# Attention and a spectral filter on one core: the filter's last feature products with the constants as weights, and results stored as whole blocks

## The chip, the cores and the metric

The program runs on one core of a Trainium2 chip. TensorE (PE) multiplies matrices, VectorE (DVE) and ScalarE (ACT) do elementwise work, GpSimd (POOL) and SyncE (SP) mostly issue DMAs. The metric is the device time of one execution in microseconds (us). It was 641.86 us in the median of three runs (641.53 to 643.83).

## The reference

Two independent results lie side by side in the output. The left half is attention of 16 heads of 28 features over 2048 positions, with one shared key and value head. The right half is a filter: a real two-dimensional Fourier transform, a product with complex weights, and the inverse transform.

```python
q = (x @ wq).reshape(B, S, 16, 28).transpose(0, 2, 1, 3)   # S = 2048, D = 448
k, v = x @ wk, x @ wv
p = softmax(einsum("bhqd,bkd->bhqk", q, k) * 28 ** -0.5)
a = (einsum("bhqk,bkd->bhqd", p, v)).transpose(0, 2, 1, 3).reshape(B, S, 448) @ wo

X = rfft2(x2) * (w_r + 1j * w_i)        # over positions and features
b = irfft2(X, s=(2048, 448))
out = concatenate([a, b], axis=-1)
```

## The kernel before

**Attention.** After a first phase (projections, the filter's forward products) the program is one long loop over 256 *steps*. A step is 128 keys against one group of four heads and 512 queries; 16 steps make a group, 16 groups make all. A step has four *scores* (`score`, L1100: keys as weights, 512 queries going through, one PSUM bank each), four exponentials on ACT (`exps`, L1117: a bank to a tile `p` in SBUF, from a pool of `P_BUFS` tiles), and four *value products* (`values`, L1132: 32 columns of the array each, two instructions per product). Value products of several steps are issued in one *batch*; `size` makes it 4 steps when other work is waiting and 2 when none is. All of a batch's tiles `p` must be there before it begins.

**Other work.** The loop puts *units* of other work between scores (`fill`): W units (`wo_mm`, L1020: the output projection, four pieces of three matmuls), and for the last part of the filter z units (L942) and y units (L961). A unit takes one of the seven PSUM banks that the scores also use, and holds it until DVE has copied the result out. A z unit multiplies four point blocks of the filtered spectrum with position constants `fi` (inverse transform over positions, eight instructions in float32); DVE copies its bank to SBUF (L948). A y unit is the inverse transform over features: four products of 113 feature constants (`cs3`), where the *points* z are the weights (128 columns) and the constants go through (113 columns), in float32, two instructions each. DVE then forms sums and differences in five operations (L966 to L975) and SP stores 128 output rows (L977). There are eight blocks q of points, with two z units and two y units each.

**What sets the order.** The order of every engine is fixed when the program is built. A planner (`clk`, `after`, `vector`, and the loop at L1189) walks through the loop with an estimated clock for PE, ACT and DVE and estimated costs per piece (the last numbers in `return [(0.88, go)]` and in `after(clk["pe"] + 1.2, 0.72, out, b)`), and writes down at each moment what its estimate allows: a score when a bank is free, a unit when its quota allows, the value products when their tiles are ready and 7 further scores (`LEAD`) are out or no bank is free. So a changed cost changes the order of everything behind it.

**Memory.** `X` (28.25 KB in each partition) holds the spectrum while DVE transforms it; it lies in a pool that is open for the whole program. After it is stored to `t2`, its space is carved up by hand for the buffers of the z and y units (`carve`, L912). The constants `cs3` are loaded into a tile of their own at the loop's start (L694).

Of the kernel before, what the change touches and what calls it, by code (L numbers as in the profile page):

```python
# [12 lines left out]
F32 = mybir.dt.float32  # L13
F32R = mybir.dt.float32r
# [3 lines left out]
ALU = mybir.AluOpType  # L18
# [4 lines left out]
S, D, H = 2048, 448, 16  # L23
# [5 lines left out]
NK = 4  # L29
SCALE = DH ** -0.5  # L30
BOUND = float(np.float32(40.0 / SCALE))
P_BUFS = 20
LEAD = 7
WARM = 8, 8
FIRST = 8
# [60 lines left out]
def kernel(ctx: ExitStack, tc: tile.TileContext, t: dict):  # L96
    nc = tc.nc
    mm = nc.tensor.matmul

    cp = ctx.enter_context(tc.tile_pool(name="cp", bufs=1))  # L100
    dp = ctx.enter_context(tc.tile_pool(name="dp", bufs=1, space=DRAM))
    qp = ctx.enter_context(tc.tile_pool(name="qp", bufs=1))
    fp = ctx.enter_context(tc.tile_pool(name="fp", bufs=2))
# [4 lines left out]
    vs = cp.tile([128, 16, 32], F32, name="vs")  # L108
    cvec = cp.tile([128, NG, NC], F32, name="cvec")
    bits = cp.tile([1, 1], F32, name="bits")  # L110
    X = cp.tile([128, 2, 32, 113], F32, name="X")
    t1 = dp.tile([64, 2, 2, 32 * 113], F32, name="t1")
    t2 = dp.tile([128, 2, 32 * 113], F32, name="t2")

    bank = [bp.tile([128, 512], F32, name=f"b{i}") for i in range(8)]
    turn = count()

    def view(b, *dims):
        n = int(np.prod(dims))
        names = "abc"[:len(dims)]  # L120
        return b[:, :n].rearrange(f"p ({' '.join(names)}) -> p {' '.join(names)}", **dict(zip(names, dims)))
# [4 lines left out]
    fc, xb, ff = {}, {}, {}  # L126
# [86 lines left out]
    with tc.tile_pool(name="f1", bufs=2) as f1[0], tc.tile_pool(name="w1", bufs=1) as w1, ExitStack() as ctx1:  # L213
# [124 lines left out]
        for j in range(NK):  # L338
            (xh_, xl_), w_ = split[0, j], wsp[j]
            if j == 0:  # L340
# [184 lines left out]
        for c in range(1, NC):  # L525
            for g in range(NG):
                n = 4 * (c - 1) + g
                m = None
                for j in range(NK):
# [4 lines left out]
                    m = add(PE, 0.2285 * (3 if j < 3 else 2), go, *split[c, j], users[-6] if j == 0 else None)  # L534
# [25 lines left out]
                if n in PLACES:  # L560
                    q = PLACES.index(n)
# [41 lines left out]
        for i in range(4):  # L603
            r = slice(32 * i, 32 * i + 32)
# [12 lines left out]
        with tc.If(rv > int(np.float32(BOUND).view(np.int32))), tc.tile_pool(name="g1", bufs=1) as g1:  # L617
# [10 lines left out]
            with tc.For_i(0, 64, 1) as n:  # L628
# [3 lines left out]
                for i in range(4):  # L632
                    r = slice(32 * i, 32 * i + 32)
# [11 lines left out]
            q, qh, ql = parts  # L645
# [14 lines left out]

    ap = ctx.enter_context(tc.tile_pool(name="ap", bufs=2))
    pp = ctx.enter_context(tc.tile_pool(name="pp", bufs=P_BUFS))
    V = nc.vector
    TT, STT = V.tensor_tensor, V.scalar_tensor_tensor

    clk = {"pe": 0.0, "dve": 4.0, "act": 0.0, "mode": "s", "new": False}
    free = [0.0] * 6 + [9.0]
# [4 lines left out]
    def after(when, dur, f, *a):  # L672
        heapq.heappush(events, (when, next(serial), dur, f, a))
# [16 lines left out]

    woh = ap.tile([128, NG, D], F32R, name="woh", bufs=1)
    wol = ap.tile([128, NG, D], F32R, name="wol", bufs=1)
    fc["cs3"] = ap.tile([113, 4, 113], F32, name="cs3", bufs=1)
    nc.gpsimd.dma_start(fc["cs3"], t["cs3"])  # L694

    late, held, early = {}, [None], deque()

# [208 lines left out]
                after(clk["dve"] + 3.0, 0.0, fft3_load, k)  # L906


    Xf = X.rearrange("p r n f -> p (r n f)")
    taken = [0]  # L910

    def carve(p, n):  # L912
        o = taken[0]
        taken[0] += n
        return Xf[:p, o:o + n]

    c2t = [carve(128, 904).rearrange("p (u j f) -> p u j f", u=2, f=113) for _ in range(2)]
    fit = [carve(128, 512).rearrange("p (j f) -> p j f", f=128) for _ in range(2)]
    zt = [[carve(113, 512).rearrange("p (r j n) -> p r j n", r=2, n=64) for _ in range(2)] for _ in range(2)]
    mt = [carve(128, 226).rearrange("p (k f) -> p k f", f=113) for _ in range(2)]  # L920
    y1t = [carve(128, 452).rearrange("p (k h f) -> p k h f", k=2, f=113) for _ in range(2)]
    yot = [carve(128, 452).rearrange("p (k f) -> p k f", f=113) for _ in range(2)]

    work = {"z": deque(), "w": deque()}
    cur, last_kind = [None], ["w"]
# [3 lines left out]
    def fft3_load(q):  # L929
        if q > 7:  # L930
            return
        nc.gpsimd.dma_start(c2t[q % 2].rearrange("p u j f -> p u (j f)"), t2[:, :, 452 * q:452 * q + 452])
        nc.gpsimd.dma_start(fit[q % 2], t["fi"][:, 4 * q:4 * q + 4])
        after(clk["dve"] + (10.0 if q < 2 else 6.0), 0.0, work["z"].extend, [z_unit(q, 0), z_unit(q, 1)])

    def z_unit(q, e):
        w = (113, 112)[e]

        def go(b):
            pz = view(bank[b], 4, 128)  # L940
            for j in range(4):
                mm(pz[:w, j], c2t[q % 2][:, e, j, :w], fit[q % 2][:, j], start=True, stop=True)  # L942
            if e == 1:
                after(clk["pe"] + 1.2, 0.0, fft3_load, q + 2)
            after(clk["pe"] + 1.2, 0.72, out, b)

        def out(b):
            V.tensor_copy(zt[q % 2][e][:w], view(bank[b], 4, 128)[:w].rearrange("p j (r n) -> p r j n", r=2))  # L948
# [3 lines left out]
        return [(0.88, go)]  # L952

    def y_unit(q, v):
        js = slice(2 * v, 2 * v + 2)

        def go(b):
            py = view(bank[b], 4, 113)
            ze, zo = zt[q % 2]
            for k, (z, w, r) in enumerate(((ze, 113, 0), (zo, 112, 0), (zo, 112, 1), (ze, 113, 1))):  # L960
                mm(py[:, k], z[:w, r, js], fc["cs3"][:w, k], start=True, stop=True)  # L961
# [150 lines left out]
    def exps():  # L1112

        while waiting and waiting[0][0] < 4 * done_steps + P_BUFS:
            i, b, at = waiting.popleft()
# [72 lines left out]
    n = size()  # L1188
    while done_steps < 256:  # L1189
# [10 lines left out]
        elif t_v <= clk["pe"] + 0.05 and (sc >= min(need + LEAD, 1024) or not soon):  # L1200
# [3 lines left out]
            n = size()  # L1204
# [15 lines left out]
        elif t_v <= min(free) or not more:  # L1220
# [3 lines left out]
            n = size()  # L1224
# [117 lines left out]
def _gather(oa, ob):  # L1342
    out = np.empty((1, S, 2 * D), np.float32)
    out[0, :, :D] = oa
    y = ob.reshape(32, 64, 4, 113).transpose(1, 0, 2, 3).reshape(S, 4, 113)
# [26 lines left out]
```

## Time and profile before

| | |
|---|---|
| median of three runs | 641.86 us |
| the profiled execution | 641.98 us |
| its span, first to last instruction | 640.1 us |
| PE, ACT, DVE busy | 633.5, 547.0, 333.3 us |
| scores L1100, 1024 instructions | 284.7 us busy, 411 ns each |
| value products L1132, 2048 instructions | 240.0 us busy, 597 ns each |
| exponentials L1117, 1024 instructions | 506.7 us busy, 768 ns each |
| y units L961, 128 instructions | 21.9 us busy |
| z units L942, 128 instructions | 16.6 us busy |
| granted TensorE clock | 0.999 |

Matmuls are pipelined: a matmul's duration in the trace is longer than the distance to the next, and a PE that is shown as busy may be waiting. So the distances between starts in the timeline say what a matmul costs, and the busy time of PE says little.

### The profile page before, as it was taken

To read this page: it belongs to the slowest core of one execution; us is meant where nothing else is said; L and a number is where in the kernel's file an instruction comes from. 1 tells how busy PE (TensorE), PEld (TensorE's weight loads), DVE (VectorE), ACT (ScalarE), POOL (GpSimd) and SP (SyncE) were. 2 spreads that over 40 slices of the span, in tenths; PEclk is the share of its full clock that TensorE was granted. 3 is DMA by queue.
4 is the path that set the end of the run, shared out by engine and by line. 5 is a ranking of instruction groups with operands and counts; after the bars stand their busy time and mean duration, and the time that the engine had idled before them with its cause. 6 is when DMAs were issued, how large, how long until landed. Compare 5 with 4: busy or idle time off the path is not lost.

```text
span 640.1 us, 11636 instructions
## 1 busy us (share of the span) xinstructions
PE 633.5 (99%) x4380; PEld 358.5 (56%) x4380; DVE 333.3 (52%) x687; ACT 547.0 (85%) x1100; POOL 89.1 (14%) x164
## 2 busy tenths in 40 slices
PE   9999999999999999999999999999999999999997
PEld 7877544444444456554446655655665655564445
DVE  5999615979897977896323222215334310320014
ACT  4644899999999998889999879878888987888991
POOL 1021131101121101010122020020301101020200
PEclk9999999999999999999999999999999999999999
DMA  8766587030334121124444231132415131130002
GB/s 299 255 164 166 134 239 244 18 68 17 97 105 102 42 68 47 32 67 150 151 141 139 64 91 36 49 111 88 115 61 143 32 82 32 50 93 1 19 0 87
DMA packets 29667, 62.41 MB, mean 98 GB/s; under 512 B 6798, under 2 KB 18415, under 8 KB 28645
## 3 DMA queue, kind: packets, MB, share of 16 engines
q1 hardware_dynamic: 21850, 40.36, 23.1%
q0 software_dynamic: 7328, 20.72, 10.8%
q8 instruction: 35, 0.57, 0.4%
q10 hardware_dynamic: 432, 0.57, 0.3%
q14 instruction: 22, 0.18, 0.1%
HBM read 29.63 MB, written 15.02 MB: 70 GB/s over the span
## 4 chain that ended last, share of the span: by engine, by line
PE 88%; ACT 0%; issue 0%; DVE 0%; ACTq 0%
PE b L1100 41%; PE b L1132 36%; PE b L1020 6%; PE b L961 2%; PE b L942 2%; PE b L1252 0%; PE b L163 0%; ACT yb L1035 0%; DVE yb L1038 0%; ACTq L1036 0%
## 5 line engine op out<-in xcount | busy, mean ns | idle before, releaser
L1117 ACT ACTIVATE p<-b 128x512 f32<-128x512 f32 x1024 | 506.7, 768 | 46.4 <-PE b L1100 45.4
L1100 PE MATMUL b<-qa,ka 128*128 128x512 f32 x1024 | 284.7, 411 | 0.5 <-PEq L617 0.5
L1100 PEld LDWEIGHTS b<-qa,ka 128*128 128x128 f32 x1024 | 182.1, 188 | 128.2 <-ACT p L1117 83.9
L1132 PE MATMUL b<-p,vs 128*32 128x512 f32 x2048 | 240.0, 597 | 0.0
L1132 PEld LDWEIGHTS b<-p,vs 128*32 128x32 f32 x2048 | 56.5, 109 | 120.9 <-issue 119.3
L986 DVE COPY qraw<-b 128x512 f32<-128x512 f32 x15 | 10.4, 692 | 82.0 <-PE b L1132 82.0
L1024 DVE COPY ya<-b 128x448 f32<-128x448 f32 x12 | 7.5, 624 | 65.1 <-PE b L1020 64.0
L991 POOL DMA_DIRECT2D sd<-qraw x15 | 8.8, 587 | 218.8 <-DVE qraw L986 218.8
L827 DVE SCALAR_TENSOR_TENSOR X<-w,X 128x226 f32<-128x226 f32 (+2 forms) x72 | 34.1, 473 | 2.4
L1000 POOL DMA_DIRECT2D R<-rd x60 | 30.2, 508 | 34.9 <-DMA rd<-rs 34.9
L966 DVE COPY X<-b 128x226 f32<-128x226 f32 x16 | 6.2, 390 | 45.3 <-ACT p L1117 43.9
L321 ACT ACTIVATE qraw<-b 128x512 f32<-128x512 f32 x16 | 9.4, 599 | 19.5 <-PE b L317 19.4
L948 DVE COPY X<-b 113x512 f32<-113x512 f32 (+1 forms) x16 | 11.1, 691 | 28.6 <-ACT p L1117 22.7
L317 PE MATMUL b<-xh,wqh 128*128 128x512 f32 x64 | 24.6, 416 | 0.4 <-DVE xh L265 0.4
L1008 DVE TENSOR_TENSOR qraw<-qraw,R 128x512 f32<-128x512 f32 x15 | 10.3, 685 | 26.7 <-DMA R<-rd 26.7
L317 PE MATMUL b<-xh,wql 128*128 128x512 f32 x64 | 23.0, 390 | 0.0
L1020 PE MATMUL b<-woh,oh 128*128 128x448 f32 x60 | 22.1, 369 | 0.0
L1020 PE MATMUL b<-wol,oh 128*128 128x448 f32 x60 | 22.0, 366 | 0.0
L1020 PE MATMUL b<-woh,ol 128*128 128x448 f32 x60 | 21.9, 366 | 0.0
L820 DVE SCALAR_TENSOR_TENSOR w<-X 128x113 f32<-128x113 f32 (+2 forms) x56 | 17.7, 353 | 0.1
L961 PEld LDWEIGHTS b<-cs,X 113*128 113x128 f32 (+1 forms) x128 | 16.8, 191 | 1.4
L317 PE MATMUL b<-xl,wqh 128*128 128x512 f32 x48 | 17.3, 391 | 0.0
(113 smaller groups left out, 511.4 us busy)
## 6 DMA issues: line engine op xcount, KB each, us to landing
qa<-qa SPq DMA_DIRECT2D x15, 512.0 KB
X<-t POOLq DMA_DIRECT2D x16, 452.0 KB, 5.4
xb<-xb SPq DMA_DIRECT2D x8, 512.0 KB
qa<-qh SPq DMA_DIRECT2D x60, 64.0 KB
qa<-ql SPq DMA_DIRECT2D x60, 64.0 KB
R<-rd POOLq DMA_DIRECT2D x60, 64.0 KB, 2.2
t<-bs SPq DMA_DIRECT2D x16, 226.0 KB
wf<-w POOLq DMA_DIRECT2D x8, 452.0 KB, 4.2
```

Source lines behind the costliest of these rows:

```text
L317: mm(pq[c, g], w[:, j, gs], x[:, j], start=(j == 0 and n == 0), stop=(j == 3 and n == 1))
L820: STT(out, y, sy, x, op0=ALU.mult, op1=ALU.add if c > 0 else ALU.subtract)
L827: todo(226 * n, lambda d=d, q=q: STT(both(d), t[0].rearrange("p r n f -> p r (n f)"), q, both(a), op0=ALU.mult, op1=ALU.add))
L942: mm(pz[:w, j], c2t[q % 2][:, e, j, :w], fit[q % 2][:, j], start=True, stop=True)
L948: V.tensor_copy(zt[q % 2][e][:w], view(bank[b], 4, 128)[:w].rearrange("p j (r n) -> p r j n", r=2))
L961: mm(py[:, k], z[:w, r, js], fc["cs3"][:w, k], start=True, stop=True)
L986: V.tensor_copy(o, bank[7])
L1000: nc.gpsimd.dma_start(R[32 * i:32 * i + 32], rd[i:i + 1].to_broadcast([32, CW]))
L1020: mm(p, x[c][:, g, s], w[:, g], start=(g == 0 and n == 0), stop=(g == NG - 1 and n == 2))
L1100: mm(bank[b], ka[:, kc * 128:(kc + 1) * 128], qa[c, g][:, h], start=True, stop=True)
L1117: nc.scalar.activation(p, bank[b], AF.Exp, scale=SCALE)
L1132: mm(bank[7][32 * i:32 * i + 32], vs[:, kc], pt.pop(4 * st + i), start=(kc == 0), stop=(kc == 15))
```

## The change

The operands of the y unit change places. Each feature constant (113 columns) becomes the weight, and the points (4 blocks of 64, 256 columns) go through. The products are in float32r instead of float32, and to keep the accuracy the constants and the points are each split into a high and a low part (`csh`, `csl`; `zh`, `zl`); one product becomes three (high by high, high by low, low by high). The two y units of a block q no longer take half of the points each, but half of the feature constants each. A unit has 6 instructions of 256 columns instead of 8 of 113.

DVE now writes two tiles per z unit (the high part by a copy, the low part by a subtraction), does three operations per y unit, and after the second unit of a block two operations of 512 columns that make the output blocks. SP stores two blocks of 113 x 512 for each q, each contiguous in DRAM; the host's `_gather` reorders accordingly.

`X` moves to a pool that is closed when the first z unit's data are loaded, and a new pool takes its space. The load of the constants moves from the loop's start to that moment, goes to a scratch tile, and two DVE operations make `csh` and `csl`. To make room, `P_BUFS` goes from 20 to 19. The planner's costs of the z and y units change.

```diff
-P_BUFS = 20
+P_BUFS = 19
...
-    X = cp.tile([128, 2, 32, 113], F32, name="X")
...
     pp = ctx.enter_context(tc.tile_pool(name="pp", bufs=P_BUFS))
+    xp = ctx.enter_context(ExitStack())
+    X = xp.enter_context(tc.tile_pool(name="xp", bufs=1)).tile([128, 2, 32, 113], F32, name="X")
...
-    fc["cs3"] = ap.tile([113, 4, 113], F32, name="cs3", bufs=1)
-    nc.gpsimd.dma_start(fc["cs3"], t["cs3"])
+    csh = ap.tile([113, 4, 113], F32R, name="csh", bufs=1)
+    csl = ap.tile([113, 4, 113], F32R, name="csl", bufs=1)
...
+    def fft3_open():
+        xp.close()
+        p3 = xp.enter_context(tc.tile_pool(name="p3", bufs=2))
+        for q in range(2):
+            fb["c2", q] = p3.tile([128, 2, 4, 113], F32, name="c2")
+            fb["fi", q] = p3.tile([128, 4, 128], F32, name="fi")
+            for e in range(2):
+                fb["z", q, e] = [p3.tile([113, 2, 4, 64], F32R, name=f"z{n}{e}") for n in "hl"]
+        cs = scratch()[:113, :452].rearrange("p (k f) -> p k f", k=4)
+        nc.gpsimd.dma_start(cs, t["cs3"])
+        todo(452, lambda: V.tensor_copy(csh, cs))
+        todo(452, lambda: TT(csl, cs, csh.bitcast(F32), op=ALU.subtract))
...
-            after(clk["pe"] + 1.2, 0.72, out, b)
+            after(clk["pe"] + 1.2, 1.4, out, b)
 
         def out(b):
-            V.tensor_copy(zt[q % 2][e][:w], view(bank[b], 4, 128)[:w].rearrange("p j (r n) -> p r j n", r=2))
+            pz = view(bank[b], 4, 128)[:w].rearrange("p j (r n) -> p r j n", r=2)
+            h, l = (x[:w] for x in fb["z", q % 2, e])
+            V.tensor_copy(h, pz)
+            TT(l, pz, h.bitcast(F32), op=ALU.subtract)
...
     def y_unit(q, v):
-        js = slice(2 * v, 2 * v + 2)
 
         def go(b):
-            py = view(bank[b], 4, 113)
-            ze, zo = zt[q % 2]
-            for k, (z, w, r) in enumerate(((ze, 113, 0), (zo, 112, 0), (zo, 112, 1), (ze, 113, 1))):
-                mm(py[:, k], z[:w, r, js], fc["cs3"][:w, k], start=True, stop=True)
-            after(clk["pe"] + 1.2, 1.2, out, b)
+            py = view(bank[b], 2, 256)
+            for k in range(2):
+                kind, e, r = ((0, 0, 0), (2, 1, 1), (1, 1, 0), (3, 0, 1))[2 * v + k]
+                w = (113, 112)[e]
+                zh, zl = (x[:w, r].rearrange("p j n -> p (j n)") for x in fb["z", q % 2, e])
+                for n, (c, z) in enumerate(((csh, zh), (csh, zl), (csl, zh))):
+                    mm(py[:113, k], c[:w, kind], z, start=(n == 0), stop=(n == 2))
+            after(clk["pe"] + 1.2, 2.65 if v else 1.25, out, b)
 
         def out(b):
-            py, m, y1 = view(bank[b], 4, 113), mt[v], y1t[v]
-            V.tensor_copy(m, py[:, 2:4])
-            TT(y1[:, :, 0], py[:, 0:2], m, op=ALU.add)
-            TT(y1[:, :, 1], py[:, 0:2], m, op=ALU.subtract)
-            free[b] = clk["dve"] + 0.1
-            after(clk["dve"], 0.8, last)
-
-        def last():
-            y1, yo = y1t[v], yot[v]
-            TT(yo[:, 0:2], y1[:, 0], y1[:, 1], op=ALU.add)
-            TT(yo[:, 2:4], y1[:, 0], y1[:, 1], op=ALU.subtract)
-            r0 = (2 * q + v) * 128
-            nc.sync.dma_start(t["ob"][r0:r0 + 128], yo)
-        return [(0.88, go)]
+            py = view(bank[b], 2, 256)[:113]
+            y = y1[v] = scratch()[:113, :768].rearrange("p (s n) -> p s n", s=3)
+            V.tensor_copy(y[:, 2], py[:, 1])
+            TT(y[:, 0], py[:, 0], y[:, 2], op=ALU.add)
+            TT(y[:, 1], py[:, 0], y[:, 2], op=ALU.subtract)
+            free[b] = clk["dve"] + (-1.3 if v else 0.1)
+            if v:
+                a, c = y1.pop(0), y1.pop(1)
+                for h, op in enumerate((ALU.add, ALU.subtract)):
+                    last(h, op, a, c)
+
+        def last(h, op, a, c):
+            yo = fp.tile([113, 2, 256], F32, name="yo", tag="bs")
+            TT(yo, a[:, :2], c[:, :2], op=op)
+            nc.sync.dma_start(t["ob"][q, h], yo)
+        return [(0.73, go)]
...
-    total = 12 * 4 * 0.605 + 32 * 0.88
+    total = 12 * 4 * 0.605 + 16 * (0.88 + 0.73)
...
-_OUTS = {"oa": (S, D), "ob": (S, 4, 113)}
+_OUTS = {"oa": (S, D), "ob": (8, 2, 113, 2, 256)}
```

**PE, y units late in the filter.** The rows are PE's instructions in program order, one row for each product or run of equal products; `b_` are PSUM banks, `qa` and `ka` the scores' operands. Before, two y units of one block stand in a loop of their own:

```order
L961 MATMUL b_79<-cs_1092,X 128x113 x4
L1100 MATMUL b_81<-qa_128,ka 128x512
L1100 MATMUL b_77<-qa_128,ka 128x512
L961 MATMUL b_78<-cs_1092,X 128x113 x4
L1100 MATMUL b_82<-qa_128,ka 128x512
L1100 MATMUL b_83<-qa_128,ka 128x512
L1100 MATMUL b_80<-qa_128,ka 128x512
```

The same place now, from the scores between the two y units on (scores are L1112, y products L971, z products L945):

```order
L1112 MATMUL b_78<-qa_1166,ka 128x512
L1112 MATMUL b_81<-qa_1166,ka 128x512
L971 MATMUL b_76<-zh_3747,csh 113x256
L971 MATMUL b_76<-zl_3748,csh 113x256
L971 MATMUL b_76<-zh_3747,csl 113x256
L971 MATMUL b_76<-zh_3745,csh 113x256
L971 MATMUL b_76<-zl_3746,csh 113x256
L971 MATMUL b_76<-zh_3745,csl 113x256
L1112 MATMUL b_77<-qa_1166,ka 128x512
L1112 MATMUL b_79<-qa_1166,ka 128x512
L945 MATMUL b_82<-fi,c_3749 112x128 x4
```

The unit has six products in place of four double ones, and behind the second y unit there now stands a z unit in the same batch.

**DVE, what takes the units out of their banks.** Before, two y units and the next block's two z units (`X` are the buffers carved from X):

```order
L966 COPY X<-b_80 128x226
L967 TENSOR_TENSOR X<-b_80,X 128x2x113
L968 TENSOR_TENSOR X<-b_80,X 128x2x113
L974 TENSOR_TENSOR X<-X 128x226
L975 TENSOR_TENSOR X<-X 128x226
L966 COPY X<-b_81 128x226
L967 TENSOR_TENSOR X<-b_81,X 128x2x113
L968 TENSOR_TENSOR X<-b_81,X 128x2x113
L974 TENSOR_TENSOR X<-X 128x226
L975 TENSOR_TENSOR X<-X 128x226
L948 COPY X<-b_79 113x512
L948 COPY X<-b_78 112x512
```

The same place now:

```order
L977 COPY w<-b_81 113x256
L978 TENSOR_TENSOR w<-b_81,w 113x256
L979 TENSOR_TENSOR w<-b_81,w 113x256
L977 COPY w<-b_78 113x256
L978 TENSOR_TENSOR w<-b_78,w 113x256
L979 TENSOR_TENSOR w<-b_78,w 113x256
L988 TENSOR_TENSOR yo<-w 113x512 x2
L953 CAST zh_3751<-b_77 113x512
L954 TENSOR_TENSOR zl_3752<-b_77,zh_3751 113x512
L953 CAST zh_3753<-b_80 112x512
L954 TENSOR_TENSOR zl_3754<-b_80,zh_3753 112x512
```

The last sums come only behind the second y unit, for both together, and each z unit has a second operation that reads its bank.

**DVE, where the transform ends.** Before, with the attention's normalisation (L1008 to L1011, which needs a tile `R` that a DMA brings) right behind a reciprocal:

```order
L827 SCALAR_TENSOR_TENSOR X<-w,X 128x2x113 x2
L996 RECIPROCAL rs<-rs 128x16
L1008 TENSOR_TENSOR qraw<-qraw,R 128x512
L1010 CAST oh<-qraw 128x512
L1011 TENSOR_TENSOR ol<-qraw,oh 128x512
```

Now:

```order
L828 SCALAR_TENSOR_TENSOR X<-w,X 128x2x113 x2
L1008 RECIPROCAL rs<-rs 128x16
L922 CAST csh<-w 113x452
L923 TENSOR_TENSOR csl<-w,csh 113x452
L1020 TENSOR_TENSOR qraw<-qraw,R 128x512
L1022 CAST oh<-qraw 128x512
L1023 TENSOR_TENSOR ol<-qraw,oh 128x512
```

The split of the constants, which waits for their DMA, stands ahead of that normalisation. In POOL's queue that DMA stands behind the four DMAs that bring `R` and ahead of the loads for the first z units.

More of the change, by code (lines that the diff above doesn't have):

```diff
@@ L906, in store @@
                 after(clk["dve"] + 3.0, 0.0, fft3_load, k)
[L909 to L922, printed above, removed]
+    fb = {}
+    def fft3_open():
[10 more added lines that the diff above has]
+        todo(452, lambda: TT(csl, cs, csh.bitcast(F32), op=ALU.subtract))
     work = {"z": deque(), "w": deque()}
@@ L931, in fft3_load @@
             return
-        nc.gpsimd.dma_start(c2t[q % 2].rearrange("p u j f -> p u (j f)"), t2[:, :, 452 * q:452 * q + 452])
-        nc.gpsimd.dma_start(fit[q % 2], t["fi"][:, 4 * q:4 * q + 4])
+        if not fb:
+            fft3_open()
+        nc.gpsimd.dma_start(fb["c2", q % 2].rearrange("p u j f -> p u (j f)"), t2[:, :, 452 * q:452 * q + 452])
+        nc.gpsimd.dma_start(fb["fi", q % 2], t["fi"][:, 4 * q:4 * q + 4])
         after(clk["dve"] + (10.0 if q < 2 else 6.0), 0.0, work["z"].extend, [z_unit(q, 0), z_unit(q, 1)])
@@ L941, in go @@
             for j in range(4):
-                mm(pz[:w, j], c2t[q % 2][:, e, j, :w], fit[q % 2][:, j], start=True, stop=True)
+                mm(pz[:w, j], fb["c2", q % 2][:, e, j, :w], fb["fi", q % 2][:, j], start=True, stop=True)
             if e == 1:
                 after(clk["pe"] + 1.2, 0.0, fft3_load, q + 2)
-            after(clk["pe"] + 1.2, 0.72, out, b)
+            after(clk["pe"] + 1.2, 1.4, out, b)
         def out(b):
-            V.tensor_copy(zt[q % 2][e][:w], view(bank[b], 4, 128)[:w].rearrange("p j (r n) -> p r j n", r=2))
+            pz = view(bank[b], 4, 128)[:w].rearrange("p j (r n) -> p r j n", r=2)
+            h, l = (x[:w] for x in fb["z", q % 2, e])
+            V.tensor_copy(h, pz)
+            TT(l, pz, h.bitcast(F32), op=ALU.subtract)
             free[b] = clk["dve"] + 0.1
@@ L952, in z_unit @@
         return [(0.88, go)]
+    y1 = {}
     def y_unit(q, v):
[L955 removed]
         def go(b):
[L958 to L978 removed]
+            py = view(bank[b], 2, 256)
[6 more added lines that the diff above has]
+            after(clk["pe"] + 1.2, 2.65 if v else 1.25, out, b)
+        def out(b):
+            py = view(bank[b], 2, 256)[:113]
[13 more added lines that the diff above has]
+        return [(0.73, go)]
     oh, ol, osb = {}, {}, {}
@@ L1344, in _gather @@
     out[0, :, :D] = oa
-    y = ob.reshape(32, 64, 4, 113).transpose(1, 0, 2, 3).reshape(S, 4, 113)
+    y = ob.reshape(8, 2, 113, 2, 4, 64).transpose(5, 0, 4, 1, 3, 2).reshape(S, 4, 113)
     d = np.arange(113)
```

## The prediction

> **What bounds the kernel now.** I read the page first, for the engines' shares, then the view of waits, then PE's timeline for the distances between starts.
>
> ```profile
> PE 633.5 (99%) x4380; PEld 358.5 (56%) x4380; DVE 333.3 (52%) x687; ACT 547.0 (85%) x1100; POOL 89.1 (14%) x164
> ACT p L1117 <- PE b L1100: 45.4, 31, 1.7
> ACT p L1117 <- PE b L1132: 1.0, 6, 0.2
> ```
>
> PE looks full, but its ends are modelled. The second row says that ACT is starved of scores 31 times, for 45.4 us; the third that it hardly ever waits for a value product to give back a tile `p`. Now two neighbouring batches of the filter's last part. A *cycle* is the time from the start of one batch of value products to the next.
>
> ```profile
> 453.96 3.64 PE L1132 MATMUL b<-p,vs 128*32 128x512 f32 x32
> 457.53 1.66 PE L1100 MATMUL b<-qa,ka 128*128 128x512 f32 x6
> 459.03 1.03 PE L942 MATMUL b<-X 128*112 128x128 f32 x8
> 459.82 0.71 PE L1100 MATMUL b<-qa,ka 128*128 128x512 f32 x2
> 460.37 1.03 PE L942 MATMUL b<-X 128*113 128x128 f32 x8
> 461.17 2.47 PE L1100 MATMUL b<-qa,ka 128*128 128x512 f32 x9
> 463.57 3.64 PE L1132 MATMUL b<-p,vs 128*32 128x512 f32 x32
> 467.14 1.67 PE L1100 MATMUL b<-qa,ka 128*128 128x512 f32 x6
> 468.64 1.04 PE L961 MATMUL b<-cs,X 113*128 113x113 f32 x8
> 469.45 0.70 PE L1100 MATMUL b<-qa,ka 128*128 128x512 f32 x2
> 470.00 1.04 PE L961 MATMUL b<-cs,X 113*128 113x113 f32 x8
> 470.81 1.95 PE L1100 MATMUL b<-qa,ka 128*128 128x512 f32 x7
> 472.68 0.64 PE L1132 MATMUL b<-p,vs 128*32 128x512 f32 x4
> ```
>
> The cycle with two z units takes 463.57 - 453.96 = 9.61 us, the one with two y units 9.11. From the starts: four steps of value products 3.57; a z unit 0.79; a y unit 468.64 to 469.45 = 0.81; two scores behind a z or y unit 0.55. The next cycle, with three W units, shows what a score costs otherwise, and where PE waits.
>
> ```profile
> 237.06 3.64 PE L1132 MATMUL b<-p,vs 128*32 128x512 f32 x32
> 243.40 0.37 PE L1020 MATMUL b<-woh,ol 128*128 128x448 f32 x1
> 243.81 0.62 PE L1100 MATMUL b<-qa,ka 128*128 128x512 f32 x2
> 244.27 0.37 PE L1020 MATMUL b<-woh,oh 128*128 128x448 f32 x1
> 244.88 1.85 PE L1100 MATMUL b<-qa,ka 128*128 128x512 f32 x6
> 246.66 3.64 PE L1132 MATMUL b<-p,vs 128*32 128x512 f32 x32
> ```
>
> Two scores behind a W unit take 0.46, so a score is 0.23, and the first score behind a float32 unit costs 0.09 more. A W product of 448 columns (float32r) takes 0.205 (243.40 to 243.81 for two). The y unit so costs PE 0.81 + 0.09 = 0.90. Six scores behind the values take 1.50: 0.12 extra for the first; seven scores before the values 1.87 = 0.09 + 7 x 0.23 + 0.17 for the turn to value products. Here the last six scores take 1.78 where 6 x 0.23 + 0.17 = 1.55 would do: PE stands 0.23 waiting for exponentials. With sixteen scores this cycle is 9.60, and ACT sets it. The rule behind it: at a batch's start PE has issued a number of scores beyond the batch, the *lead* (6 or 7, counted in the order). During the 3.57 us of values ACT works off the lead and starves; then it needs the other 16 - 6 = 10 exponentials one by one.
>
> ```profile
> 458.07 8.44 ACT L1117 ACTIVATE p<-b 128x512 f32<-128x512 f32 x17 [1.66 <-PE b L1100]
> 150.86 1.92 PE L1132 MATMUL b<-p,vs 128*32 128x512 f32 x16
> 154.79 1.92 PE L1132 MATMUL b<-p,vs 128*32 128x512 f32 x16
> 588.67 1.92 PE L1132 MATMUL b<-p,vs 128*32 128x512 f32 x16
> 592.62 1.92 PE L1132 MATMUL b<-p,vs 128*32 128x512 f32 x16
> ```
>
> ACT's pace is 3.93 / 8 = 0.49 per exponential (a bare cycle of two steps, lead 7; 3.95 with lead 6). So ACT's floor for four steps is 9.60 with lead 6, and 9.60 - 0.49 = 9.11 with lead 7; less the values and the exponentials, 9.60 - 3.57 - 10 x 0.49 = 1.13 is the latency from the last value product through the first score. The cycle of two y units has lead 7: its PE sum, 3.57 + 1.50 + 0.81 + 0.55 + 0.81 + 1.87 = 9.11, stands exactly at ACT's floor. **PE and ACT are bound together**, so a cheaper y unit in an unchanged order would gain nothing there; what it can do is let the planner pack the units into fewer long cycles.
>
> **The y unit.** Six products of 256 columns, float32r. The nearest rows are 0.205 for 448 columns and 0.23 for 512 in the same type: in proportion 256 columns are 0.117, on the line through both 0.205 - 192 x 0.025 / 64 = 0.13. I take 0.1225, so 0.735 for the unit, and no 0.09 behind it, since W units, of the same type, show none. Against 0.90 it saves 0.165, in 16 units 2.6 us of PE time (bounds 3.2 and 1.9). The loads of the weights must hide behind a stream of that length:
>
> ```profile
> L961 PEld LDWEIGHTS b<-cs,X 113*128 113x128 f32 x64 | 10.9, 190 | 1.4
> L942 PEld LDWEIGHTS b<-X 128*113 128x113 f32 x64 | 8.1, 177 | 0.8
> ```
>
> A load of 113 columns is recorded with 177 ns, but in the z unit eight of them with their products pass in 0.79, one in 0.099. So the record is a latency, and 0.1225 has room. [...]
>
> **The order that follows.** I counted the cycles in PE's order before and after, by steps before and in the cycle. They are alike until the first y unit. 2 to 2 steps: 64 before, 64 after. 4 to 4: 27 and 21. 2 to 4: 3 and 7. 4 to 2: 3 and 7. The pattern is "y, y, z" in one batch where "y, y" and "z, z" alternated. Prices for the short kinds:
>
> ```profile
> 332.37 1.93 PE L1132 MATMUL b<-p,vs 128*32 128x512 f32 x16
> 340.76 0.64 PE L1132 MATMUL b<-p,vs 128*32 128x512 f32 x4
> 510.09 3.64 PE L1132 MATMUL b<-p,vs 128*32 128x512 f32 x32
> 515.96 1.92 PE L1132 MATMUL b<-p,vs 128*32 128x512 f32 x16
> 519.86 1.92 PE L1132 MATMUL b<-p,vs 128*32 128x512 f32 x16
> 527.52 1.06 PE L1132 MATMUL b<-p,vs 128*32 128x512 f32 x8
> ```
>
> 2 to 4: 8.39 with W, z, z; 7.66 with three W units. 4 to 2: 5.87 with nine scores, one score less 5.64. Long cycles: gone are five at 9.60, four at 9.11 and one (W, z, z, 17 scores) with a PE sum of 10.1, together 94.5. New are two of y, W, W at 9.45 and two of y, y, z, whose PE sum is 3.57 + 1.50 + 2 x 0.735 + 2 x 0.46 + 0.79 + (0.09 + 6 x 0.23 + 0.17) = 9.89, together 38.7: -55.9. New 2 to 4: one at 7.66; two of y, y, z at 9.89 - 1.72 = 8.17 (two steps of values fewer: 3.64 against 1.92 in the rows); one with two scores fewer, at ACT's 16 x 0.49 = 7.84: +31.8. New 4 to 2: two at 5.87, one at 5.64, one with lead 5 at 3.57 + 1.13 + 3 x 0.49 = 6.17: +23.6. Ten bare cycles go from lead 6 to 7 (-0.2), and the last cycle loses a W piece (-0.2). Sum **-0.9 us**; each price is good to some 0.02, which leaves ±0.4, and the y bounds make it -1.5 to 0.0.
>
> **What costs nothing, and its cover.** z units: DVE's second operation doubles the time a bank is held.
>
> ```profile
> L948 DVE COPY X<-b 113x512 f32<-113x512 f32 (+1 forms) x16 | 11.1, 691 | 28.6 <-ACT p L1117 22.7 <-PE b L942 5.9
> 319.01 1.98 POOL L1000 DMA_DIRECT2D R<-rd  x4 [7.62 <-DMA rd<-rs]
> 322.85 0.69 DVE L1008 TENSOR_TENSOR qraw<-qraw,R 128x512 f32<-128x512 f32 x1 [12.86 <-DMA R<-rd]
> 334.36 0.69 DVE L986 COPY qraw<-b 128x512 f32<-128x512 f32 x1 [7.99 <-PE b L1132]
> cs<-cs POOLq DMA_DIRECT2D x1, 199.5 KB, 3.6
> ```
>
> It goes from 0.69 to 1.38, 11 us more DVE in all. The bank of the first z unit is next written by the fifth score after it: 0.55 + 0.79 + 0.09 + 4 x 0.23 = 2.35 after its end; DVE needs some 0.35 to start and 1.38. Margin 0.6, so nothing, while DVE is free. The y units' five operations of 226 and the new three of 256 plus half of two of 512 are about the same work. The constants' DMA is issued behind R's, at 320.98, and lands 3.6 later with its 0.5 of issue at about 325; DVE stands for it, and the normalisation behind it begins some 3 us later than 322.85. DVE's next work, the bank of 334.36, leaves 8 us: covered. The loads for the z units move 0.6 later, far from their use at 336. `P_BUFS` 19: at a batch of four steps at most 16 + 7 scores are out, so the twentieth exponential waits for the first step, 0.9 into the values; the four left then end at 2.9, before the values do at 3.57. Covered by 0.7, and bare cycles never have 19 out. The stores are as many bytes on SP, off the path.
>
> **Rivals.** (1) *PE alone counts*: if ACT's floor is not where I put it, the 2.6 us come in full, up to 3.2, and with the bare cycles 3.6: about 638.9. For it: the z cycle has only 0.07 of wait. Against: the 0.23 in the W cycle. (2) *No gain*: ACT's pace carries everything, 641.8; for it the floor in the y cycle, against it the new packing. (3) Slower: *DVE holds the banks*. If a z unit finds DVE inside a y unit's tail (3 x 0.42 + 1.38 = 2.64), its bank comes back later than the 2.35, and PE stands; it decides from 0.6 us of lateness on. At 0.5 us per z unit in eight to ten cycles +4 to +5: about 645.2. Against it: "y, y, z" has a batch of values (3.57) before that bank's next use. (4) Slower: *loads not hidden*. At 177 ns per product a unit is 1.06, 0.33 over mine, in 16 units +5.2: about 646. [...] Against it the z unit's 0.099.
>
> **Chances.** Forecast 0.52; (1) 0.15; (2) 0.13; (3) 0.12; (4) 0.08, of which 0.02 for the full price. About 0.5%, 3.2 us, can be told from no change here. Below 638.65 lies half of (1) and a little of the forecast's edge: faster 0.11. Above 645.07 lie (4), most of (3) and a little else: slower 0.19. Same 0.70. The profiled execution stands 0.12 above the median (641.98; 640.1 of span and 1.9 around it); its change is added to the median: 641.86 - 0.9 = **640.96**, rounded 641.0. The range goes from full PE gain to most of (3): 638.8 to 645.2.
>
> **What would show it.** y products start 0.12 apart, and the two scores behind them take 0.46; the y, y, z cycle is near 9.9, and cycles with lead 6 stay at 9.60. Bare cycles are 3.93. Wrong: y products 0.18 apart (4), scores behind z or y units that wait for DVE (3), a cycle of lead 7 below 9.1 (1), or DVE later than 334 at the constants.

## The result: 2.4% slower, and where the time went

The changed kernel takes 657.7 us in the median of six runs (656.9 to 657.8), the kernel before 641.9 on the same chip: a ratio of 1.024, 95% interval 1.0225 to 1.0257. The forecast was 641.0. The profiled execution has a span of 655.9 against 640.1. First the page of the changed kernel: its engines, the chain that ended last, and the group of DVE operations that make the output blocks (the last field of a group is the idle time of its engine just before it, with its releaser).

```profile
span 655.9 us, 11600 instructions
PE 638.0 (97%) x4348; PEld 357.4 (54%) x4348; DVE 346.3 (53%) x689; ACT 549.5 (84%) x1100; POOL 88.6 (14%) x164
...
PE 73%; DMA 14%; DVE 1%; issue 1%; ACT 0%; ACTq 0%; DVEq 0%
PE b L1112 35%; PE b L1144 30%; DMA ob<-yo 14%; PE b L1032 6%; PE b L945 1%; PE b L971 1%; PE b L1264 0%; DVE zh L953 0%; DVE zl L954 0%; PE b L162 0%; DVE yo L988 0%; ACT yb L1047 0%; DVE w L977 0%; DVE w L979 0%; DVE qraw L1020 0%
...
L988 DVE TENSOR_TENSOR yo<-w 113x512 f32<-113x512 f32 x16 | 10.7, 691 | 23.1 <-DMA ob<-yo 22.8
```

The busy times moved little: PE +4.5, ACT +2.5, DVE +13 (11.1 of it the second operation of the z units, L954). What is new is in the chain: 14% of the span is a transfer, the store `ob<-yo` of the output blocks. The view of waits names who stands for it, and who stands behind that.

```profile
DVE yo L988 <- DMA ob<-yo: 22.8, 4, 6.8
...
PE b L1112 <- DVE zl L954: 10.8, 4, 4.1
```

DVE stands four times, 22.8 us in all, before it may write a block `yo`, until the store that still reads that buffer is done. PE's scores stand four times for `zl`, the operation with which DVE empties the bank of a z unit. DVE's and PE's timelines show that the two are one event.

```profile
453.50 0.69 DVE L988 TENSOR_TENSOR yo<-w 113x512 f32<-113x512 f32 x1
460.08 0.69 DVE L988 TENSOR_TENSOR yo<-w 113x512 f32<-113x512 f32 x1 [5.88 <-DMA ob<-yo]
460.69 0.68 DVE L953 CAST zh<-b 113x512 fp32r<-113x512 f32 x1
461.40 0.69 DVE L954 TENSOR_TENSOR zl<-b,zh 113x512 fp32r<-113x512 f32 x1
```

```profile
454.81 3.64 PE L1144 MATMUL b<-p,vs 128*32 128x512 f32 x32
458.38 0.97 PE L1112 MATMUL b<-qa,ka 128*128 128x512 f32 x3
462.15 0.97 PE L1112 MATMUL b<-qa,ka 128*128 128x512 f32 x3 [2.80 <-DVE zl L954]
...
466.90 1.50 PE L1144 MATMUL b<-p,vs 128*32 128x512 f32 x12
```

DVE writes the first block of a pair at 453.50, and stands before the second for 5.88 us. The z unit's bank waits behind it in DVE's order: `zh` and `zl` end at 462.09. After the values PE issues three scores of the six that come there, needs the bank, and goes on at 462.15. The cycle takes 466.90 - 454.81 = 12.09 us instead of 9.1. The worst places are later:

```profile
482.01 3.64 PE L1144 MATMUL b<-p,vs 128*32 128x512 f32 x32
...
490.60 2.18 PE L1112 MATMUL b<-qa,ka 128*128 128x512 f32 x5 [4.06 <-DVE zl L954]
492.72 2.74 PE L1144 MATMUL b<-p,vs 128*32 128x512 f32 x16
...
501.61 3.64 PE L1144 MATMUL b<-p,vs 128*32 128x512 f32 x32
...
509.85 1.65 PE L1112 MATMUL b<-qa,ka 128*128 128x512 f32 x3 [3.71 <-DVE zl L954]
...
516.97 1.50 PE L1144 MATMUL b<-p,vs 128*32 128x512 f32 x12
```

Here cycles of 5.63 and 9.10 (as they are without the wait, in the first experiment below) take 10.71 and 15.36. Six cycles are longer: those that start at 454.8, 472.8, 482.0, 492.7, 501.6 and 530.6, by 3.0, 1.0, 5.1, 0.8, 6.3 and 0.4, together 16.6 us. The one behind them is 0.4 shorter, so 16.2 remain.

**Why the store is slow.** A block was 128 rows of 452 columns before; now it is 113 rows of 512, with exactly as many bytes (226.0 KB). The next fences have the same view, the windows, for a stretch after such a pair of stores is issued: before, then after. After the five engines come the granted clock, the share of the 16 DMA engines that is busy, and GB/s.

```profile
434.50:439.50 5.00, 5.00 (x39) 1.82 (x38) 3.05 (x8) 3.36 (x8) 0.00 (x0) 1.00 0.25 93
```

```profile
438.00:444.00 6.00, 6.00 (x39) 4.41 (x31) 2.71 (x5) 4.69 (x10) 1.04 (x2) 1.00 0.06 18
```

0.06 is one sixteenth: one DMA engine's worth of work in six microseconds, at 18 GB/s. The single packets in the trace's DMA records say the same:

```
before, both stores: 256 packets of 1808 bytes from 435.10 to 439.19, 32 completion writes (16 for each store)
after, first block:  113 packets of 2048 bytes from 438.40 to 450.54, in single file, 1 completion write at 450.62
                     (443.05 to 447.45: one every 0.080 us)
after, second block: first packet at 450.62, completion write at 459.70
```

The second block begins when the first is done. It is one engine that works in single file there, and not the whole queue of SP: SP issues seven loads of `qa` meanwhile (32 rows, so 32 packets, each), and of these 224 packets 210 run beside the second block. Only two packets and one completion write of each load come behind the block, from 459.71 to 460.87, again 0.08 us apart. A pair of blocks takes at least 2 x 113 x 0.080 = 18.1 us there. There are two buffers `yo`, one for each block of a pair: where the next pair comes less than that later, DVE finds one still being read. Here SP issues the stores of a pair at 437.63, and DVE makes the next pair from 453.50 on, 15.87 later: the first buffer is free since 450.62, the second is not.

```profile
437.63 2.90 SPq L989 DMA_DIRECT2D ob<-yo  x2
```

The completion writes are read here as the number of engines that a transfer has: the store of 128 rows has 16 of them, in a stretch with a DMA share of 0.25; the store of 113 rows has one, with a share of 0.06; and of each load of 32 rows, what stands behind the block is 2 packets and one write, a sixteenth of the load. 113 is a prime. The theory that the experiments test, called the *divisor rule* below, is that a transfer issued by SP goes to as many engines as the largest number up to 16 that divides its rows: 16 for 128 rows, one for 113.

### The profile page after: what moved, and what is told of

It is laid out like the page before. It is cut to its first block, busy times and chain, and to the rows that moved or that the text cites. A ratio compares the mean times of both kernels' runs of the same rounds, so it can differ in the third digit from the quotient of the medians.

```text
span 655.9 us, 11600 instructions
## 1 busy us (share of the span) xinstructions
PE 638.0 (97%) x4348; PEld 357.4 (54%) x4348; DVE 346.3 (53%) x689; ACT 549.5 (84%) x1100; POOL 88.6 (14%) x164
## 2 busy tenths in 40 slices
DMA packets 29186, 62.40 MB, mean 95 GB/s; under 512 B 6558, under 2 KB 16127, under 8 KB 28165
## 4 chain that ended last, share of the span: by engine, by line
PE 73%; DMA 14%; DVE 1%; issue 1%; ACT 0%; ACTq 0%; DVEq 0%
PE b L1112 35%; PE b L1144 30%; DMA ob<-yo 14%; PE b L1032 6%; PE b L945 1%; PE b L971 1%; PE b L1264 0%; DVE zh L953 0%; DVE zl L954 0%; PE b L162 0%; DVE yo L988 0%; ACT yb L1047 0%; DVE w L977 0%; DVE w L979 0%; DVE qraw L1020 0%
## 5 line engine op out<-in xcount | busy, mean ns | idle before, releaser
L1112 PE MATMUL b<-qa,ka 128*128 128x512 f32 x1024 | 287.9, 413 | 11.8 <-DVE zl L954 10.8
L1112 PEld LDWEIGHTS b<-qa,ka 128*128 128x128 f32 x1024 | 182.6, 189 | 138.8 <-ACT p L1129 92.6
L988 DVE TENSOR_TENSOR yo<-w 113x512 f32<-113x512 f32 x16 | 10.7, 691 | 23.1 <-DMA ob<-yo 22.8
L953 DVE CAST zh<-b 113x512 fp32r<-113x512 f32 (+1 forms) x16 | 11.0, 689 | 15.9 <-PE b L945 7.4
L977 DVE COPY w<-b 113x256 f32<-113x256 f32 x16 | 6.8, 423 | 23.1 <-PE b L971 22.7
L945 PEld LDWEIGHTS b<-fi,c 128*112 128x112 f32 (+1 forms) x128 | 17.5, 191 | 2.2 <-ACT p L1129 0.6
L1009 POOL DMA_DIRECT2D rd<-rs x15 | 8.2, 550 | 76.5 <-DVE rs L1008 63.9
## 6 DMA issues: line engine op xcount, KB each, us to landing
t<-bs SPq DMA_DIRECT2D x16, 226.0 KB
```

The costliest lines, as they stand in the source:

```text
L945: mm(pz[:w, j], fb["c2", q % 2][:, e, j, :w], fb["fi", q % 2][:, j], start=True, stop=True)
L953: V.tensor_copy(h, pz)
L988: TT(yo, a[:, :2], c[:, :2], op=op)
L1112: mm(bank[b], ka[:, kc * 128:(kc + 1) * 128], qa[c, g][:, h], start=True, stop=True)
```

## Experiments

**The store cut in 112 rows and one.** Only the division of the transfer changes; all the rest of the change stays.

```diff
             TT(yo, a[:, :2], c[:, :2], op=op)
-            nc.sync.dma_start(t["ob"][q, h], yo)
+            for r in (slice(0, 112), slice(112, 113)):
+                nc.sync.dma_start(t["ob"][q, h, r], yo[r])
```

> The changed kernel, each block stored as 112 rows and 1 row instead of 113 at once. Theory (slow store): a DMA of 113 rows runs on one of the 16 DMA engines, because 113 has no divisor, two of them need about 20 us, and DVE waits for their buffers. Then no wait of yo for ob is left, the long stalled cycles (12.1, 10.7, 15.4 us) go back to 9.1, 5.7, 9.1 and the time is 640.3 to 641.5 us. Rival (banks): PE stalls because DVE holds the banks of the z units twice as long; then the stalled cycles stay and the time is above 652 us.

Measured: 642.3 us (640.2 to 647.1, twelve runs) against 643.4 of before on the same chip, ratio 0.9992 (0.9967 to 1.0017). The time lies above the 640.3 to 641.5 that was expected, as the kernel before does there (643.4 against 641.9 in the first comparison); the rest of the expectation came. DVE's wait for `ob<-yo` and PE's for `zl` are gone from the view of waits. The windows after a pair of stores and PE's timeline over two cycles of this kernel:

```profile
441.00:447.00 6.00, 6.00 (x39) 4.48 (x31) 2.70 (x6) 4.80 (x11) 1.16 (x2) 1.00 0.24 77
```

```profile
447.92 3.64 PE L1145 MATMUL b<-p,vs 128*32 128x512 f32 x32
451.50 1.66 PE L1113 MATMUL b<-qa,ka 128*128 128x512 f32 x6
453.00 0.28 PE L971 MATMUL b<-zh,csh 113*113 113x256 f32 x1
453.12 0.28 PE L971 MATMUL b<-zl,csh 113*113 113x256 f32 x1
...
453.71 0.62 PE L1113 MATMUL b<-qa,ka 128*128 128x512 f32 x2
454.17 0.28 PE L971 MATMUL b<-zh,csh 112*113 112x256 f32 x1
...
457.70 3.64 PE L1145 MATMUL b<-p,vs 128*32 128x512 f32 x32
...
466.80 3.64 PE L1145 MATMUL b<-p,vs 128*32 128x512 f32 x32
```

The cycle with two z units, which took 12.09 in the changed kernel, takes 466.80 - 457.70 = 9.10. From here on kernels are also compared by their *loop*, the distance from the first batch of value products to the last, because the time before it differs between executions, also of kernels that are alike up to there (last section). The two rows that give it, before, after, and with the cut:

```profile
76.31 1.92 PE L1132 MATMUL b<-p,vs 128*32 128x512 f32 x16
...
624.04 1.92 PE L1132 MATMUL b<-p,vs 128*32 128x512 f32 x16
```

```profile
77.38 1.92 PE L1144 MATMUL b<-p,vs 128*32 128x512 f32 x16
...
639.78 1.92 PE L1144 MATMUL b<-p,vs 128*32 128x512 f32 x16
```

```profile
80.30 1.92 PE L1145 MATMUL b<-p,vs 128*32 128x512 f32 x16
...
626.48 1.92 PE L1145 MATMUL b<-p,vs 128*32 128x512 f32 x16
```

547.73, 562.40 and 546.18. The division of the store is worth 16.2 us, more than the loop's whole loss of 14.7; the rest of the change is a gain of 1.5 us.

**The slow store alone, in the kernel before.** 127 is a prime too; the two transfers carry the same bytes as before.

```diff
-            nc.sync.dma_start(t["ob"][r0:r0 + 128], yo)
+            for r in (slice(0, 127), slice(127, 128)):
+                nc.sync.dma_start(t["ob"][r0 + r.start:r0 + r.stop], yo[r])
```

> The kernel before with its own result stores cut into 127 rows and 1 row, and nothing else. Theory (slow store): 127 has no divisor either, one store takes about 10 us on one DMA engine, two of a block 20 us where blocks come every 18.7 us in the filter's last part, so DVE waits for the output buffers and the kernel loses 2 to 10 us. Rival (banks, or the new operations of DVE): no change, 641.5 to 642.2 us.

Measured: 659.6 us (658.8 to 660.1, four runs), ratio 1.0256 (1.0222 to 1.0289); loop 564.75, 17.0 more than before. The direction was as expected, the size larger: DVE stands in six places, for 39.3 us, where the changed kernel has four and 22.8. The expectation had put a pair of blocks at 20 us on one engine, with 18.7 between pairs; in the DMA records two pairs in file take 44.5 us (512 packets, 465.21 to 509.75), 22 each, so the lag is larger. In its view of waits L974 is the DVE operation that writes the block, L948 and L968 empty banks of z and y units, L1101 are the scores:

```profile
DVE X L974 <- DMA ob<-X: 39.3, 6, 7.8
...
PE b L1101 <- DVE X L968: 6.7, 2, 3.7
...
PE b L1101 <- DVE X L948: 5.2, 2, 3.9
```

So the wait needs nothing of the new products: a slow store behind two buffers makes it in the old kernel too. This kernel's trace has 6574 packets under 512 bytes, which completion writes of 4 bytes are, against 6798 before: 224 fewer, as many as go when each of the sixteen stores has two completion writes (127 rows and 1) instead of 16.

**The same 113 rows, issued by POOL.** One transfer per block again, from another queue.

```diff
-            nc.sync.dma_start(t["ob"][q, h], yo)
+            nc.gpsimd.dma_start(t["ob"][q, h], yo)
```

> The changed kernel with the blocks' stores issued by POOL instead of SP, still 113 rows in one transfer. Theory: what stalls the kernel is that a 113-row transfer issued by SP goes through one DMA engine, a packet of 2048 bytes every 0.08 us, 9 us a block. [...] Then DVE's wait of 22.8 us for the previous block's store goes, and the time is that of the kernel with the store cut in 112 and 1: 641 to 644 us, 0.996 to 1.002 of before. Rival: one engine whatever issues it, as 113 is a prime: the wait stays at 20 us or more and the time at 656 to 659 (1.022 to 1.026). Second rival: POOL is late with the issue, because it stands behind other transfers in its order: 645 to 650, with a wait of some us on the store at the same place.

Measured: 642.0 us (640.1 to 645.4, ten runs) against 642.8, ratio 0.9993 (0.997 to 1.0016); loop 621.87 - 75.60 = 546.27, that of the kernel with the cut. Its list of DMA issues (the last number is the median time to landing) and its waits; POOL now stands for the blocks, at no cost to the loop:

```profile
ob<-yo POOLq DMA_DIRECT2D x16, 226.0 KB, 3.2
```

```profile
POOL ob L989 <- DVE yo L988: 81.1, 8, 16.5
```

A store lands 3.2 us after its issue; the two of the pair above, from SP, landed 13 and 21 us after theirs (437.63 to 450.62, 438.23 to 459.70). DVE no longer waits. The theory held, and both rivals fell: what the 113 rows cost depends on the queue that issues them. In the DMA records a pair of stores from POOL is 112 packets of 4096 bytes (two rows) and two with a single row, all begun between 437.24 and 439.55. How POOL's queue deals them out to engines was not shown. One word would have mended the change.

**How rows go to engines.** Each pair of blocks is cut in another way.

```diff
-            nc.sync.dma_start(t["ob"][q, h], yo)
+            o = 0
+            for n in {0: (113,), 1: (112, 1), 2: (104, 9), 3: (98, 15), 4: (108, 5), 5: (96, 17), 6: (88, 25), 7: (80, 33)}[q]:
+                nc.sync.dma_start(t["ob"][q, h, o:o + n], yo[o:o + n])
+                o += n
```

> The changed kernel with each block's store cut in another way: 113 rows for the first pair of blocks, then 112+1, 104+9, 98+15, 108+5, 96+17, 88+25 and 80+33. It measures how rows go to DMA engines on SP's queue. [...] Only the first pair can hold DVE; the time is 641 to 648. Rival: only rows that divide by 16 are spread, all else goes through one engine: 104, 98, 108 and 88 rows take 8.3, 7.8, 8.6 and 7.0 us, DVE waits for the store at four or five places more, and the time is 650 to 657.

Measured: one run, 643.9 us, with no wait of DVE for a store. Three pairs stand alone on their queue, so that their completion writes can be counted (226 packets of 2048 bytes each time):

| cut | completion writes counted | by the divisor rule, two blocks | if only multiples of 16 were spread |
|---|---|---|---|
| 104 + 9 | 44 | 2 x (13 + 9) = 44 | 2 x (1 + 1) = 4 |
| 108 + 5 | 34 | 2 x (12 + 5) = 34 | 4 |
| 96 + 17 | 34 | 2 x (16 + 1) = 34 | 34 |

The divisor rule fits all three and its rival two of them not at all. The pair cut in 104 and 9 takes 2.2 us from first to last packet; its four transfers, issued one after another from 440.23 on, are under way together. Only the 17 rows, with one completion write, show the clean spacing, 0.08 to 0.09 us at the end of their pair. The other five pairs share their stretch with loads or stand behind one. The pair cut in 98 and 15 has 74 writes with one load of `qa` (64 rows; 16 writes where it stands alone in the traces of before and after) beside it, which leaves 58 = 2 x (14 + 15). Over the whole execution there are 6834 packets under 512 bytes, 276 more than the 6558 of the changed kernel; by the rule the sixteen blocks have 292 completion writes instead of 16, also 276 more. The uncut first pair goes in single file as before, but the next pair comes over 50 us later, so nothing waits.

**The planner's old price for y units, with the cut.** This asks whether the gain comes from cheaper products alone.

```diff
-        return [(0.73, go)]
+        return [(0.88, go)]
...
-    total = 12 * 4 * 0.605 + 16 * (0.88 + 0.73)
+    total = 12 * 4 * 0.605 + 32 * 0.88
```

> The kernel of the split store, with the planner told the old price of a y unit (0.88), so that the order of PE is near that of before while the y unit really takes 0.73. Theory (PE and ACT bound together, the gain comes only through the order): 641.3 to 642.2 us, no gain over before. Rival (PE alone counts): 16 units save 2.6 us whatever the order, 639 to 639.8 us.

Measured: 644.4 us (641.6 to 647.0), ratio 1.0015 (0.9994 to 1.0035); loop 548.3, 0.6 more than before. The products are as cheap as with the cut alone, yet the loop is 2.1 us longer. It is not the order of before either (56 bare cycles of two steps instead of 62, and five that go from two steps to four with two y units), so it shows that the order decides over the gain, but not what the new products would give in the old order.

**One tile `p` less, in the kernel before.**

```diff
-P_BUFS = 20
+P_BUFS = 19
```

> The kernel before with 19 tiles p instead of 20 and nothing else. Theory: ACT hardly waits for tiles, 641.5 to 642.2 us, the same as before. Rival (fewer tiles cost part of what was lost): 643 us or more.

Measured: 643.3 us (641.1 to 644.6), ratio 0.9997 (0.9979 to 1.0016). The time lies above the 641.5 to 642.2 that was expected, but so does the kernel before on this chip (643.4). It costs nothing: the loop is 547.70 against 547.73.

**Packing further.** Two versions of the kernel with the cut let the planner put more units into one batch.

```diff
-        return max(1.6, n * (total - done[0]) / max(250 - done_steps, 3)) if n > 2 else 0.0
+        return max(2.2, n * (total - done[0]) / max(250 - done_steps, 3)) if n > 2 else 0.0
```

> The kernel with the store cut in 112 and 1, and the planner's least share of other work in a batch of four steps raised from 1.6 to 2.2 us, so that three units go into a batch more often and more batches are bare ones of two steps. Theory (the prediction's pricing of cycles, 3.93 us for a bare two-step cycle, the larger of PE's sum and ACT's floor else): the last loop 544.3 us, against 546.2 with the store cut alone and 547.7 before; 640.0 us, ratio to before 0.994 to 0.998. Rival: a third unit in a batch is paid in full, since the exponentials after it come later and its bank is given back later (DVE has two or three pieces behind each unit): the loop 546 to 549, ratio 0.999 to 1.003.

The second has besides:

```diff
-        rich = sum(map(len, work["w"])) * 0.6 + len(work["z"]) * 0.88 + (len(cur[0][0]) * 0.6 if cur[0] else 0.0) > 1.0
+        rich = sum(map(len, work["w"])) * 0.6 + len(work["z"]) * 0.88 + (len(cur[0][0]) * 0.6 if cur[0] else 0.0) > 2.0
```

> As the kernel with the least share 2.2, and the planner takes four steps only where over 2.0 us of other work stands ready (1.0 before). Theory: the last loop 542.9 us, and six W products more behind it (6 x 0.205 = 1.2 us): 639.9 us in all, ratio to before 0.993 to 0.998; level with the former within 0.5 us. Rival: units that wait longer make DVE's work come in bursts, banks come free late: ratio 0.999 to 1.004.

Measured against 642.8 of before: 640.9 us (638.5 to 643.5, twelve runs), ratio 0.9969 (0.9945 to 0.9994), and 640.4 us (638.7 to 644.2, twelve runs), ratio 0.9964 (0.9943 to 0.9984). The loops, first for the least share of 2.2 alone:

```profile
80.67 1.92 PE L1145 MATMUL b<-p,vs 128*32 128x512 f32 x16
...
625.02 1.92 PE L1145 MATMUL b<-p,vs 128*32 128x512 f32 x16
```

```profile
77.01 1.92 PE L1145 MATMUL b<-p,vs 128*32 128x512 f32 x16
...
620.91 1.92 PE L1145 MATMUL b<-p,vs 128*32 128x512 f32 x16
```

544.35, where 544.3 was expected, and 543.90, where 542.9 was. The second looks better than it is: as was expected, six W products more stand behind its end, and what follows the loop takes 17.15 us there (638.07 - 620.91) against 16.08 with the least share alone (641.10 - 625.02). With the time behind the loop, before has 563.8, the two versions 560.4 and 561.1. Both are faster than before, by 0.3 and 0.4% in the medians with intervals that just exclude 1; they can't be told from each other. Two neighbouring long cycles of the second, with three W units and one z unit each, show the principle:

```profile
388.50 3.64 PE L1145 MATMUL b<-p,vs 128*32 128x512 f32 x32
398.82 3.64 PE L1145 MATMUL b<-p,vs 128*32 128x512 f32 x32
409.01 3.64 PE L1145 MATMUL b<-p,vs 128*32 128x512 f32 x32
414.65 1.92 PE L1145 MATMUL b<-p,vs 128*32 128x512 f32 x16
```

They take 10.32 and 10.19 us, 0.6 to 0.7 more than a cycle with three units, and other cycles are left without units: two steps to two without any are 75 and 74 in these versions, 62 with the cut alone. ACT's floor is paid in a long cycle anyway, so it pays to fill it.

## Why the prediction was wrong

The failed step is a sentence at the end of the part on what costs nothing: "The stores are as many bytes on SP, off the path." The bytes are the same, and SP has the time; but the number of rows was not asked about, and the store is on the path, because DVE waits for its buffer. It costs 16.2 us (562.40 against 546.18), eighteen times the gain that the sum forecast (0.9). No term of the sum and no rival had it. What could have told it: the change turns a block's 128 rows into 113, its number of buffers stays two, and DVE has z banks to empty behind the block. The prediction asked for each transfer how many bytes it has and when it is issued, but for the store not when it ends and who waits for the buffer.

Point by point:

- **The y unit.** Forecast 0.1225 a product; measured 0.12, and 0.71 for the six (453.00 to 453.71 above). The two scores behind it take 0.46, as forecast: no 0.09 behind float32r products. The weight loads are hidden, though each is recorded with 176 to 178 ns, and rival (4) fell. No run shows the full price, for which 0.02 of the chances stood: six loads of 0.177 and six products of 0.12, one after the other, would be 1.8 us by an estimate from these records, and the six products pass with their loads in 0.71.
- **PE and ACT bound together, and the sum.** Shown by the kernel with the cut, cycle by cycle. The starts are from PE's timeline:

| cycle | forecast | with the cut |
|---|---|---|
| y, y, z from four steps to four | 9.89 | 9.78, 9.81 |
| y, y, z from two to four | 8.17 | 8.20, 8.09 |
| the same with two scores fewer | 7.84 | 7.74 |
| y, W, W | 9.45 | 9.60, 9.60 |
| four to two, nine scores; eight; lead 5 | 5.87; 5.64; 6.17 | 5.87; 5.63 to 5.68; 6.16 |
| z, z with lead 7 | 9.11 | 9.10 |
| bare | 3.93 | 3.92 |

  The sum was -0.9, between -1.5 and 0.0; measured -1.5 in the loop, at the edge. Most of the difference is one term. The last cycle, which loses a W piece and has one score instead of two, was put at -0.2, and went from 3.74 us (620.30 to 624.04) to 2.88 (623.60 to 626.48); the rows that end it are in the loops above, these begin it:

```profile
620.30 1.92 PE L1132 MATMUL b<-p,vs 128*32 128x512 f32 x16
```

```profile
623.60 1.92 PE L1145 MATMUL b<-p,vs 128*32 128x512 f32 x16
```

  The other misses nearly cancel, and that is luck. The five y, y, z cycles came out 0.34 below their prices together, with the product at 0.1225. The two y, W, W cycles were priced 0.15 too low each: they have lead 7, so neither PE's sum nor the floor of 9.11 gives 9.60. The load of the last score waits there for a bank that ACT has yet to free, so ACT sets this cycle too, by a bound that the prediction did not have:

```profile
409.35 0.19 PEld L1113 LDWEIGHTS b<-qa,ka 128*128 128x128 f32 x1 [0.31 <-ACT p L1130]
```

- **Rival (1), PE alone counts.** It fell: 1.5 us came, not 2.6 to 3.6, and cycles at ACT's floor (9.60 with lead 6, 9.10 with lead 7) did not get shorter. With the planner's old price the products are as cheap, and the loop even grew by 0.6. **Rival (2), no gain,** fell by the same 1.5: loops of one order repeat within 0.1 us from execution to execution (547.73 and 547.70 before, 546.18 and 546.27 with the slow store mended, one profiled execution of each kernel). In the medians 1.5 us can't be told from none (0.9992, 0.9967 to 1.0017).
- **Rival (3), DVE holds the banks.** The sign that was named for it came, scores that wait for DVE behind z units, and the time moved its way, though to 657.7 and not to 645.2. Its cause did not: the y unit's tail of 2.64 us is the same with the cut, and there no score waits for `zl`. DVE was late because it stood for a store.
- **Covers that held.** `P_BUFS` 19 (the run above). The constants: DVE makes `csh` at 325.06, and is at the bank of the next group at 335.40, 258.02 us after the loop's start (77.38); before it was 334.36 - 76.31 = 258.05:

```profile
325.06 0.40 DVE L922 CAST csh<-w 113x452 fp32r<-113x452 f32 x1 [14.01 <-DMA w<-cs]
...
335.40 0.69 DVE L998 COPY qraw<-b 128x512 f32<-128x512 f32 x1 [5.85 <-PE b L1144]
```

- **The margin of 0.6 for a z unit's second DVE operation** held too: with the cut, no score waits for it.

## What to carry to other kernels

Where a change alters the shape of a transfer, price it by its number of rows as well as its bytes: ask how many DMA engines it gets and when its last packet lands (here 113 rows from SP had one completion write and took 12.2 us, where 128 rows had 16), and who waits for its buffer, however far off the path the transfer was. In an engine's fixed order such a wait becomes one for everything queued behind it; here DVE's 22.8 us for a store off the path held PSUM banks, and through them TensorE, whose scores waited 10.8 us for `zl`. A DMA share of 0.06 over some microseconds, one sixteenth, is how it looks in a profile.

## What the runs showed of the hardware that was not expected

- A 113-row transfer from SP went through one DMA engine (one completion write, a DMA share of 0.06), 2048 bytes every 0.080 us over long stretches (26 GB/s), with a few packets up to 0.53 us apart: 12.2 us for 226 KB from the first packet to the completion. The second one went to the same engine, behind it, while loads from SP went through the others. The same transfer from POOL landed in 3.2 us, with its issue.
- The time before the loop differs between executions, by more than any gain here: 4.7 us between two. The windows of 60 to 76 us of two kernels that are alike up to there, the one with the store on POOL and the one with the cut:

```profile
60.00:76.00 16.00, 14.68 (x229) 10.12 (x231) 14.10 (x30) 11.77 (x24) 1.03 (x2) 1.00 0.55 138
```

```profile
60.00:76.00 16.00, 14.96 (x239) 10.52 (x233) 13.34 (x30) 10.33 (x20) 2.23 (x5) 0.84 0.49 115
```

  The granted clock is 1.00 in the first and 0.84 in the second, and the loop starts at 75.60 and 80.30; from there on they are level within 0.1 us (546.27 and 546.18). So the distance within the loop tells half a microsecond where medians of twelve runs, spread over as much as 7 us, do not. Why the clock is lowered in some executions stays open.
